# Converting float64 weights in place and between the parts of the attention: retention and a PReLU block on one core

## The chip, the cores and the metric

The kernel runs on one core of a Trainium2 chip. The metric is device time in microseconds: the median of the runs shown, and for the profiled execution its own time and its span (first to last instruction). Engines are TensorE (PE; its weight loads PEld), VectorE (DVE), ScalarE (ACT), GpSimd (POOL) and SyncE (SP), which here issues all transfers.

## The reference

```python
# q, k, v: (8, 8, 576, 64) float32: batch, heads, positions, head size
scores = q @ k.T / sqrt(64)
gamma = 1 - 2 ** (-5 - h)                       # one per head h
ret = scores * where(i >= j, gamma ** (i - j), 0)
x = (ret @ v)  rearranged to (4608, 512)        # batch*position, head*size
h = x @ w_in                                    # w_in (512, 2048), float64
g = max(h, 0) + alpha * min(h, 0)               # alpha (2048)
out = float32(g @ w_out)                        # w_out (2048, 512), float64
```

`w_in` and `w_out` arrive as float64 and are turned into float32 on the chip by integer operations on their two halves. All matrix products are float32.

## The kernel before

**Attention.** Work goes in 16 "couples" n: a batch b and four heads (u = 0 or 1), each with 4 blocks of 128 positions and a remainder of 64. Decay is put into `q` and `v` by tables (`tab`, `tabr`), products on GpSimd (L311, L313), so that scores need only a triangular mask. A couple runs `transposes` (TensorE `pt`, `ptr`, copied by ScalarE to `kT`, `qT`, `rT`), `scores` (`ps`, `psr`, masked by VectorE into `at`, `atr`), `states` (`pu`, added up by VectorE in `sums`) and `values` (`pv`, `pvr`, copied by ScalarE into `xb`).

**MLP.** A unit is 256 tokens (block kb) by a pair of 128-wide slices of the hidden layer (i = 0 to 7): 16 matmul records `ph` (L268), VectorE's PReLU and combinations `neg`, `g` (L276 to L284), 14 records `po` (L256) with a seven-product scheme. There are 18 x 8 = 144 units. `po` of a unit is issued after `ph` of the next. The last unit of a block ends in `out_block`, which combines the seven products and stores 256 rows. Units are taken from `queue` at three places of a couple; couples 2 and 3 take 2 and 4, couples 0 and 1 none, later ones what has become ready.

**Weights.** They come in 32 pieces of 512 KB, eight (a "stage": four of `w_in`, four of `w_out`) in each of couples 0 to 3. A piece is loaded to `raw` (three buffers), then: ScalarE takes Abs of the high words (L197, `wa`) and converts the low words (L199, `wl`); GpSimd clamps `wa` (L201); VectorE shifts it into the PSUM tile `wc` (L205) and joins it with the sign bits into `wb` (L207); GpSimd adds `wb` and `wl` into the weight tile (L209). After two `w_out` pieces, four subtractions (L222: two on VectorE, two on GpSimd) form the combined weights.

**What sets the order.** The program text gives priorities, a scheduler orders each engine's queue at build time, and each queue runs in order. Buffers rotate: pool `ps_a` has three PSUM buffers, shared by `pt`, `ptr`, `ps`, `psr`, `pu`, `pv`, `pvr` and every `wc`. All eight pieces of a stage are issued between `states` and `values`. The function around these lines, as it stands before:

Of the kernel before, what the change touches and what calls it, by code (L numbers as in the profile page):

```python
# [18 lines left out]
def kernel(  # L19
# [79 lines left out]
    pbi = const.tile([P, NBIT], INT32, name="pbi")
    for i in range(NBIT):  # L100
        nc.vector.tensor_scalar(pbi[:, i:i + 1], pint, i, 1,
                                ALU.logical_shift_right, ALU.bitwise_and)
# [3 lines left out]
    facr = const.tile([P, 2, NC2, 2], FP32, name="facr")
    gpw = const.tile([P, NBIT, H], FP32, name="gpw")
    for h in range(H):
        for i in range(NBIT):
            nc.gpsimd.memset(gpw[:, i, h:h + 1], float(np.float32(gam[h] ** 2 ** i)) - 1.0)  # L110
    for h in range(H):
        for j in range(NJ):
            nc.vector.memset(fac[:, 0, j, h:h + 1], gam[h] ** (j * C - MID) / np.sqrt(D))
            nc.vector.memset(fac[:, 1, j, h:h + 1], gam[h] ** (MID - j * C))
    for u in range(NC2):
        for i in range(2):
            for h2 in range(2):
                g_ = gam[4 * u + 2 * i + h2]
                rows = slice(i * REM, (i + 1) * REM)
                at_ = NJ * C - i * REM - MID  # L120
                nc.gpsimd.memset(facr[rows, 0, u, h2:h2 + 1], g_ ** at_ / np.sqrt(D))
                nc.gpsimd.memset(facr[rows, 1, u, h2:h2 + 1], g_ ** -at_)
    pw = const.tile([P, 2, H], FP32, name="pw")
    pwt = const.tile([P, H], FP32, name="pwt")
    for i in range(NBIT):
        t_ = pw[:, 0, :] if i == 0 else pwt
        nc.vector.tensor_scalar(t_, gpw[:, i, :], pbit[:, i:i + 1], 1.0, ALU.mult, ALU.add)
        if i:
            nc.vector.tensor_tensor(out=pw[:, 0, :], in0=pw[:, 0, :], in1=pwt, op=ALU.mult)
    nc.vector.reciprocal(pw[:, 1, :], pw[:, 0, :])  # L130
# [3 lines left out]
    for x in range(2):  # L134
        for u in range(NC2):
            hs = slice(4 * u, 4 * u + 4)
            nc.vector.tensor_tensor(out=tab[x][:, u], in0=fac[:, x, :, hs],
                                    in1=pw[:, x:x + 1, hs].to_broadcast([P, NJ, 4]),
                                    op=ALU.mult)
        for i in range(2):  # L140
            rows = slice(i * REM, (i + 1) * REM)
            nc.vector.tensor_tensor(
                out=tabr[rows, x], in0=facr[rows, x],
                in1=pw[rows, x].rearrange("p (u i h) -> p u i h", u=NC2, i=2)[:, :, i, :],
                op=ALU.mult)
# [317 lines left out]
```

## Time and profile before

| | us |
|---|---|
| median of 3 runs (lowest, highest) | 1233.37 (1233.04, 1235.24) |
| profiled execution | 1234.44 |
| its span | 1232.7 |
| TensorE busy | 1134.6 (92%) |
| VectorE, GpSimd, ScalarE busy | 565.1, 191.1, 112.5 |

The profile's page gives busy shares over 40 slices of 30.8 us; TensorE's are low in the first six and full after that, GpSimd's are high in the first six and low after that. A busy share over the whole span therefore says little about the first 190 us, and that stretch is read from views of its own: busy time by stretch, waits, groups of instructions and single rows in order of time. In those rows the number after a line and an operation is what the profile holds for it: "x32" instructions, busy time, mean in ns, and idle time of the engine before them with its releaser.

### The profile page before, as it was taken

To read this page: it belongs to the slowest core of one execution; us is meant where nothing else is said; L and a number is where in the kernel's file an instruction comes from. 1 tells how busy PE (TensorE), PEld (TensorE's weight loads), DVE (VectorE), ACT (ScalarE), POOL (GpSimd) and SP (SyncE) were. 2 spreads that over 40 slices of the span, in tenths; PEclk is the share of its full clock that TensorE was granted. 3 is DMA by queue.
4 is the path that set the end of the run, shared out by engine and by line. 5 is a ranking of instruction groups with operands and counts; after the bars stand their busy time and mean duration, and the time that the engine had idled before them with its cause. 6 is when DMAs were issued, how large, how long until landed. Compare 5 with 4: busy or idle time off the path is not lost.

```text
span 1232.7 us, 16093 instructions
## 1 busy us (share of the span) xinstructions
PE 1134.6 (92%) x6529; PEld 984.7 (80%) x6529; DVE 565.1 (46%) x1535; ACT 112.5 (9%) x283; POOL 191.1 (16%) x226
## 2 busy tenths in 40 slices
PE   2236779999999999999999999999999999999998
PEld 2135658888888888888888888888888888888887
DVE  5445565534535444454453444444444444444344
ACT  1242321000000000000000000000000000000000
POOL 5977862000000000000000000000000000000000
PEclk9567889999999999999999999999999999999999
DMA  7555431101011111111010111111110000000000
GB/s 174 152 164 150 131 103 41 35 20 40 23 31 40 37 39 37 25 33 37 22 35 20 39 37 39 37 39 38 39 38 13 6 1 18 1 17 18 1 18 18
DMA packets 127146, 55.58 MB, mean 45 GB/s; under 512 B 116304, under 2 KB 116320, under 8 KB 127072
## 3 DMA queue, kind: packets, MB, share of 16 engines
q1 hardware_dynamic: 127072, 54.56, 16.6%
q8 instruction: 51, 0.84, 0.3%
q14 instruction: 23, 0.19, 0.0%
HBM read 45.10 MB, written 9.44 MB: 44 GB/s over the span
## 4 chain that ended last, share of the span: by engine, by line
PE 86%; POOL 5%; DVE 3%; DMA 2%; SPq 2%; issue 1%; ACT 1%; DVEq 0%; POOLq 0%; ACTq 0%
PE ph L268 40%; PE po L256 34%; POOL wa L201 3%; PE ps L342 3%; PE pv L394 2%; PE pt L324 2%; PE pv L385 2%; DMA raw<-in_moe_w_in_dram 2%; PE pu L365 1%; SPq L76 1%; DVE at L346 1%; POOL w_out L209 1%; SPq L81 1%; PE psr L353 1%; DVE wb L207 1%
## 5 line engine op out<-in xcount | busy, mean ns | idle before, releaser
L268 PE MATMUL ph<-xb,w_in 128*128 128x256 f32 x2304 | 538.7, 385 | 17.1 <-DVE g L278 17.1
L268 PEld LDWEIGHTS ph<-xb,w_in 128*128 128x128 f32 x2304 | 436.1, 192 | 79.9 <-DVE g L278 12.1
L256 PE MATMUL po<-w_out,g 128*128 128x256 f32 x2016 | 458.5, 379 | 0.0
L256 PEld LDWEIGHTS po<-w_out,g 128*128 128x128 f32 x2016 | 383.0, 190 | 52.1
L276 DVE TENSOR_SCALAR neg<-ph,alpha 128x256 f32<-128x256 f32 x288 | 126.3, 479 | 522.5 <-PE ph L268 522.5
L284 DVE TENSOR_TENSOR g<-g 128x128 f32<-128x128 f32 x576 | 156.1, 311 | 8.7
L278 DVE SCALAR_TENSOR_TENSOR g<-ph,neg 128x512 f32<-128x512 f32 x144 | 99.5, 691 | 4.9
L313 POOL TENSOR_TENSOR vn<-vn,tab 128x1024 f32<-128x1024 f32 x16 | 30.4, 1903 | 428.1 <-DMA vn<-in_v_dram 337.7
L385 PE MATMUL pv<-at,vn 128*64 128x128 f32 x512 | 37.7, 306 | 52.0 <-DVE wb L207 52.0
L385 PEld LDWEIGHTS pv<-at,vn 128*64 128x64 f32 x512 | 32.3, 155 | 58.7 <-issue 49.9
L313 POOL TENSOR_TENSOR qn<-qn,tab 128x1024 f32<-128x1024 f32 x16 | 30.6, 1913 | 273.4 <-DMA qn<-in_q_dram 240.6
L201 POOL TENSOR_SCALAR wa<-wa 128x512 f32<-128x512 f32 x32 | 61.3, 1920 | 16.9 <-ACT wa L197 16.9
L346 DVE TENSOR_TENSOR at<-ps,mask 128x512 f32<-128x512 f32 x64 | 41.2, 686 | 43.9 <-PE ps L342 43.9
L303 ACT COPY xb<-pv 128x256 f32<-128x256 f32 (+3 forms) x88 | 21.8, 322 | 394.4 <-PE pv L394 394.3
L342 PE MATMUL ps<-qT,kT 64*128 64x128 f32 x512 | 48.0, 285 | 3.0 <-DVE at L346 1.5
L342 PEld LDWEIGHTS ps<-qT,kT 64*128 64x128 f32 x512 | 41.9, 187 | 11.0 <-DVE at L346 6.0
L327 ACT COPY kT<-pt 128x512 f32<-128x512 f32 x32 | 17.8, 592 | 296.6 <-PE pt L324 296.4
L205 DVE TENSOR_SCALAR wc<-wa 128x512 int32<-128x512 int32 x32 | 21.9, 692 | 42.7 <-POOL wa L201 42.7
L239 ACT COPY s<-po 128x256 f32<-128x256 f32 x18 | 6.7, 372 | 326.8 <-PE po L256 326.8
L374 DVE TENSOR_TENSOR sums<-pu,sums 64x128 f32<-64x128 f32 x96 | 27.7, 289 | 2.8
L394 PE MATMUL pv<-qT,sums 128*128 128x128 f32 x192 | 28.3, 302 | 0.0
L394 PEld LDWEIGHTS pv<-qT,sums 128*128 128x128 f32 x192 | 25.1, 209 | 3.1 <-issue 3.1
(64 smaller groups left out, 432.1 us busy)
## 6 DMA issues: line engine op xcount, KB each, us to landing
out_dram<-osb SPq DMA_DIRECT2D x36, 256.0 KB, 2.2
qn<-in_q_dram SPq DMA_DIRECT2D x64, 128.0 KB, 2.7
kn<-in_k_dram SPq DMA_DIRECT2D x64, 128.0 KB, 2.8
vn<-in_v_dram SPq DMA_DIRECT2D x64, 128.0 KB, 2.8
raw<-in_moe_w_in_dram SPq DMA_DIRECT2D x16, 512.0 KB, 4.5
raw<-in_moe_w_out_dram SPq DMA_DIRECT2D x16, 512.0 KB, 4.3
qr<-in_q_dram SPq DMA_DIRECT2D x32, 32.0 KB, 2.3
kr<-in_k_dram SPq DMA_DIRECT2D x32, 32.0 KB, 2.1
```

Source lines behind the costliest of these rows:

```text
L201: nc.gpsimd.tensor_scalar(a, a, HI_MIN, HI_MAX, ALU.max, ALU.min)
L256: nc.tensor.matmul(acc[kb][n // 2][:, n % 2, :], g[:, x, :], w_out[i][:, y, :], start=(i == 0 and n % 2 == 0), stop=(i == NU - 1 and (n % ...
L268: nc.tensor.matmul(ph[:, x, :], w_in[i // UST][:, cc, x, f0:f0 + P], xb[kb][:, cc, :], start=(cc == 0), stop=(cc == NCC - 1))
L276: nc.vector.tensor_scalar(neg[:, x], ph[:, x], 0.0, alpha[:, fc:fc + 1], ALU.min, ALU.mult)
L278: nc.vector.scalar_tensor_tensor(out=g[:, 0:4, :].rearrange("p x t -> p (x t)"), in0=ph.rearrange("p x t -> p (x t)"), scalar=0.0, in1=neg ...
L284: nc.vector.tensor_tensor(out=g[:, o, :], in0=g[:, x, :], in1=g[:, y, :], op=op)
L313: nc.gpsimd.tensor_tensor(out=t, in0=t, in1=tab[x][:, u, :, :, None].to_broadcast([P, NJ, 4, D]), op=ALU.mult)
L342: nc.tensor.matmul(ps[h2][:, cols], kT[i][rows, cols], qT[i][rows, cols], start=True, stop=True)
L346: nc.vector.tensor_tensor(out=a, in0=ps[h2].rearrange("p (j w) -> p j w", w=C), in1=mask[:, None, :].to_broadcast([P, NJ, C]), op=ALU.mult)
L374: nc.vector.tensor_tensor(out=sm[hd, j, :, hd], in0=ps[hd, j, :, :], in1=sm[hd, j - 1, :, hd], op=ALU.add)
L385: nc.tensor.matmul(pv[i][h2 * D:(h2 + 1) * D, j * C:(j + 1) * C], vn[:, j, 2 * i + h2, :], at[2 * i + h2][:, j, :], start=(j == 0), stop=F ...
L394: nc.tensor.matmul(pv[i][:, j * C:(j + 1) * C], sm[:, j - 1, i, :], qT[i][:, j * C:(j + 1) * C], start=False, stop=(j == NJ - 1), skip_gro ...
```

## The change

- A piece keeps its low words in `raw` (ScalarE writes them back in place), the clamp is VectorE's, the join writes into the weight tile, and GpSimd adds the low words there. `wb` and `wl` are gone; `raw` has four buffers, `wa` three.
- The pieces stand in a list, and a couple issues two after `transposes`, three after `scores` (and the first units) and three after `values`.
- The decay tables come from repeated squares and products on VectorE, where single memsets stood on VectorE and GpSimd; the remainder mask is built on GpSimd.
- `k` is loaded before `q`. The output tiles take the `raw` and `wa` buffers, both halves of a block in one tile.

```diff
-        for name, src in (("q", q), ("k", k), ("v", v)):
+        for name, src in (("k", k), ("q", q), ("v", v)):
...
+    for i in range(NBIT):
+        nc.vector.scalar_tensor_tensor(out=dif[:, i + 1], in0=dif[:, i], scalar=2.0,
+                                       in1=dif[:, i], op0=ALU.add, op1=ALU.mult)
...
-        raw = wraw.tile([P, 2, HM, 2], INT32, tag="raw", bufs=3, name=f"raw_{at}")
+        raw = wraw.tile([P, 2, HM, 2], INT32, tag="raw", bufs=4, name=f"raw_{at}")
         nc.sync.dma_start(raw, src)
...
+        lo, hi = raw[:, :, :, 0], raw[:, :, :, 1]
+        a = wraw.tile([P, 2, HM], FP32, tag="wa", bufs=3, name=f"wa_{at}")
+        nc.scalar.activation(a, hi.bitcast(FP32), ACTF.Abs)
+        nc.scalar.activation(lo, lo.bitcast(UINT32), ACTF.Copy, scale=2.0 ** -29)
-        nc.gpsimd.tensor_scalar(a, a, HI_MIN, HI_MAX, ALU.max, ALU.min)
+        nc.vector.tensor_scalar(a, a, HI_MIN, HI_MAX, ALU.max, ALU.min)
...
-        nc.vector.scalar_tensor_tensor(out=bi, in0=flat[:, :, 1], scalar=-0x40000000, in1=c,
-                                       op0=ALU.bitwise_and, op1=ALU.bitwise_or)
-        nc.gpsimd.tensor_tensor(out=dst.bitcast(INT32),
-                                in0=bi.rearrange("p (x f) -> p x f", x=2),
-                                in1=l.rearrange("p (x f) -> p x f", x=2), op=ALU.add)
+        nc.vector.scalar_tensor_tensor(
+            out=dst.rearrange("p x f -> p (x f)").bitcast(INT32),
+            in0=raw.rearrange("p x f two -> p (x f) two")[:, :, 1], scalar=-0x40000000,
+            in1=c.rearrange("p x f -> p (x f)"), op0=ALU.bitwise_and, op1=ALU.bitwise_or)
+        nc.gpsimd.tensor_tensor(out=dst.bitcast(INT32), in0=dst.bitcast(INT32), in1=lo,
+                                op=ALU.add)
...
+    def load_weights(n):
+        for _ in range(min(n, len(pieces))):
+            src, dst, unit = pieces.pop(0)
+            load_piece(src, dst)
+            if unit is not None:
+                combine(unit)
...
-        osb = [wraw.tile([P, 2, HM], FP32, tag="wa", name=f"osb{m}_{kb}") for m in range(2)]
-        s12 = wraw.tile([P, 2, HM], FP32, tag="wb", name=f"s12_{kb}")
-        u3 = wraw.tile([P, HM], FP32, tag="wl", name=f"u3_{kb}")
+        osb = wraw.tile([P, 2, 2, HM], FP32, tag="raw", bufs=4, name=f"osb_{kb}")
+        s12 = wraw.tile([P, 2, HM], FP32, tag="wa", bufs=3, name=f"s12_{kb}")
+        u3 = wraw.tile([P, HM], FP32, tag="wa", bufs=3, name=f"u3_{kb}")
...
         qT, kT, rT = transposes(n, b, u, tiles)
+        load_weights(2)
         pop_units(share // 3)
         at = scores(n, qT, kT, rT)
+        load_weights(3)
         states(n, tiles)
-        if n < NST:
-            load_stage(n)
         pop_units(share // 3)
         values(n, b, u, tiles, qT, rT, at)
+        load_weights(3)
         pop_units(share - 2 * (share // 3))
```

How the queues change, at three places. VectorE in couple 1, before, from the last remainder product (`atr`) on; `wc` and `wb` are the two vector steps of a piece, `sums` the states:

```order
L355 TENSOR_TENSOR atr_1_677<-psr_1_675,maskr 128x128
L205 TENSOR_SCALAR wc_712<-wa_706 128x512
L205 TENSOR_SCALAR wc_724<-wa_718 128x512
L372 COPY sums<-pu_679 64x2x64 x2
L374 TENSOR_TENSOR sums<-pu_679,sums 64x2x64 x6
L207 SCALAR_TENSOR_TENSOR wb_707<-raw_704,wc_712 128x512
```

The same engine in couple 1 of the changed kernel, from the end of the second piece on (L193 is the clamp, `wa` its tile, `at` the masked scores):

```order
L199 SCALAR_TENSOR_TENSOR w_in_186<-raw_516,wc_522 128x512
L193 TENSOR_SCALAR wa_564<-wa_564 128x512
L193 TENSOR_SCALAR wa_574<-wa_574 128x512
L349 TENSOR_TENSOR at_1_536<-ps_1_526,mask 128x512
L349 TENSOR_TENSOR at_1_538<-ps_1_527,mask 128x512
L193 TENSOR_SCALAR wa_584<-wa_584 128x512
L349 TENSOR_TENSOR at_1_550<-ps_1_540,mask 128x512
L349 TENSOR_TENSOR at_1_552<-ps_1_541,mask 128x512
```

Two pieces now end ahead of the masked scores and three clamps stand among them, where all of a couple's pieces followed the scores before.

SyncE, before, between the end of couple 0 and couple 1 (loads of couple 2's `k` and `v`, and the first pieces of stage 1):

```order
L76 DMA kn_0_590<-in_k_dram 128x4x64 x4
L81 DMA kr_0_591<-in_k_dram 64x2x64 x2
L189 DMA raw_704<-in_moe_w_in_dram 128x2x512
L76 DMA vn_0_598<-in_v_dram 128x4x64 x4
L81 DMA vr_0_599<-in_v_dram 64x2x64 x2
L189 DMA raw_716<-in_moe_w_in_dram 128x2x512
```

SyncE in the changed kernel, at the same place:

```order
L76 DMA kn_0_445<-in_k_dram 128x4x64 x4
L76 DMA vn_0_461<-in_v_dram 128x4x64 x4
L81 DMA vr_0_462<-in_v_dram 64x2x64 x2
L186 DMA raw_506<-in_moe_w_in_dram 128x2x512
L186 DMA raw_516<-in_moe_w_in_dram 128x2x512
```

The first piece of the stage stood ahead of `vn` and `vr`; now it stands behind them.

TensorE, before, from the end of couple 3's values to the first transpose of couple 4 (`ph_5` is the sixth unit, `g_4` the fifth unit's PReLU):

```order
L399 MATMUL pvr_1433<-rT_1187,sums 128x64 x2
L268 MATMUL ph_5_1493<-xb_568,w_in_308 128x256 x4
L256 MATMUL po_0_1144<-w_out_314,g_4_1477 128x256 x2
L256 MATMUL po_0_1145<-w_out_314,g_4_1477 128x256 x2
L256 MATMUL po_0_1146<-w_out_314,g_4_1477 128x256 x2
L256 MATMUL po_0_1147<-w_out_314,g_4_1477 128x256
L324 MATMUL pt_4_1551<-ident,kn_0_1163 128x128 x4
```

TensorE in the changed kernel, at the same place:

```order
L402 MATMUL pvr_1210<-rT_1018,sums 128x64 x2
L259 MATMUL po_0_975<-w_out_192,g_3_1192 128x256 x2
L259 MATMUL po_0_976<-w_out_192,g_3_1192 128x256 x2
L259 MATMUL po_0_977<-w_out_192,g_3_1192 128x256 x2
L259 MATMUL po_0_978<-w_out_192,g_3_1192 128x256
L327 MATMUL pt_4_1366<-ident,kn_0_986 128x128 x4
```

The sixth unit's `ph` and the fifth unit's `po` have moved behind couple 4's transposes.

## Rows read from the trace of the kernel before

**Rows 1.** Busy time by stretch: PE, PEld, DVE, ACT, POOL, PEclk, DMA share, GB/s

```profile
0.00:62.84 62.84, 16.74 (x140) 14.81 (x140) 29.08 (x131) 15.34 (x26) 44.40 (x112) 0.72 0.62 161
62.84:104.22 41.38, 16.65 (x143) 14.18 (x144) 17.81 (x34) 16.74 (x32) 35.44 (x26) 0.62 0.53 158
104.22:143.75 39.53, 27.70 (x183) 22.02 (x184) 22.30 (x47) 12.96 (x26) 30.47 (x22) 0.81 0.50 141
143.75:194.46 50.71, 41.19 (x259) 34.02 (x259) 32.56 (x63) 13.50 (x32) 35.06 (x28) 0.90 0.39 105
194.46:1226.00 1031.54, 1030.04 (x5802) 898.01 (x5801) 460.65 (x1253) 53.58 (x169) 45.70 (x40) 1.00 0.10 27
```

**Rows 2.** Waits of 20 to 195 us: who waited for whom, total, times, longest

```profile
PE pv L385 <- DVE wb L207: 52.0, 5, 26.0
```

**Rows 3.** Waits of SyncE's queue, 20 to 190 us

```profile
SPq L189 <- DVE wb L207: 60.6, 23, 5.2
```

**Rows 4.** Groups of instructions, 20 to 195 us: busy us, mean ns, idle before

```profile
L201 POOL TENSOR_SCALAR wa<-wa 128x512 f32<-128x512 f32 x32 | 61.3, 1920 | 16.9 <-ACT wa L197 16.9
...
L205 DVE TENSOR_SCALAR wc<-wa 128x512 int32<-128x512 int32 x32 | 21.9, 692 | 42.7 <-POOL wa L201 42.7
L207 DVE SCALAR_TENSOR_TENSOR wb<-raw,wc 128x512 int32<-128x512 int32 x32 | 21.6, 683 | 1.8 <-POOL w_in L209 1.2
...
L209 POOL TENSOR_TENSOR w_in<-wb,wl 128x512 int32<-128x512 int32 x16 | 20.1, 1270 | 4.3 <-DVE wb L207 4.3
...
L284 DVE TENSOR_TENSOR g<-g 128x128 f32<-128x128 f32 x24 | 11.8, 517 | 0.3
...
L346 DVE TENSOR_TENSOR at<-ps,mask 128x512 f32<-128x512 f32 x15 | 9.7, 685 | 16.3 <-PE ps L342 16.3
...
L374 DVE TENSOR_TENSOR sums<-pu,sums 64x128 f32<-64x128 f32 x24 | 6.9, 289 | 0.7
L276 DVE TENSOR_SCALAR neg<-ph,alpha 128x256 f32<-128x256 f32 x12 | 5.5, 478 | 6.4 <-PE ph L268 6.4
...
L278 DVE SCALAR_TENSOR_TENSOR g<-ph,neg 128x512 f32<-128x512 f32 x6 | 4.1, 690 | 0.2
```

**Rows 5.** Single instructions in order of time: start, duration, engine, line

```profile
4.07 1.21 DVE L127 TENSOR_SCALAR pwt<-gpw,pbit 128x8 f32<-128x8 f32 x1
...
4.29 0.97 POOL L158 MEMSET sums<- 128x1024 f32 x1
...
5.53 0.23 DVE L152 COPY maskr<-mask 128x128 f32<-128x128 f32 x1
...
46.48 1.90 POOL L313 TENSOR_TENSOR qn<-qn,tab 128x1024 f32<-128x1024 f32 x1
...
46.56 2.10 DVE L222 TENSOR_TENSOR w_out<-w_out 128x256 f32<-128x256 f32 x1 [0.54 <-POOL w_out L209]
...
50.70 0.43 DVE L222 TENSOR_TENSOR w_out<-w_out 128x256 f32<-128x256 f32 x1 [1.44 <-POOL w_out L209]
```

**Rows 6.** Tile `raw` (ns: min/median/max, first and last start), and one stretch

```profile
L197 ACT ACTIVATE wa<-raw x32: 658/668/711, 27.3 to 179.0; 128x512 f32<-128x512 f32 x32
...
L189 SPq DMA_DIRECT2D raw<-in_moe_w_in_dram x16: 540/567/612, 22.8 to 163.6; - x16
...
DMA to landing us min/median/max: 3.2/4.4/7.2
...
20.00:30.00 10.00, 2.64 (x46) 2.15 (x46) 4.43 (x14) 1.44 (x3) 4.18 (x3) 0.87 0.82 225
```

**Rows 7.** TensorE in order of time, and on the chain of work

```profile
13.70 0.26 PE L164 MATMUL aps<-ident,a 16*128 16x16 f32 x1 [13.70 <-DMA a<-in_moe_alpha_dram]
...
59.37 2.93 PE L394 MATMUL pv<-qT,sums 128*128 128x128 f32 x12
...
203.25 3.45 PE ph L268 x16
206.70 3.02 PE po L256 x14
```

More of the change, by code (lines that the diff above doesn't have):

```diff
@@ new lines @@
+    for h in range(H):
+        nc.vector.memset(dif[:, 0, h:h + 1], gam[h] - 1.0)
+    for h in range(H):
+        nc.vector.memset(fac[:, 0, h:h + 1], gam[h] ** -MID / np.sqrt(D))
+    for i in range(NBIT):
+        nc.vector.scalar_tensor_tensor(out=dif[:, i + 1], in0=dif[:, i], scalar=2.0,
+                                       in1=dif[:, i], op0=ALU.add, op1=ALU.mult)
+    facl = const.tile([P, 2, H], FP32, name="facl")
+    for o, y, i in [(fac[:, j], fac[:, j - 1], NBIT) for j in range(1, NJ)] + \
+            [(facl[:, i], fac[:, NJ - 1], NBIT - i) for i in range(2)]:
+        nc.vector.scalar_tensor_tensor(out=o, in0=dif[:, i], scalar=1.0, in1=y,
+                                       op0=ALU.add, op1=ALU.mult)
@@ L98 @@
+    nc.vector.tensor_tensor(out=pbi, in0=pint, in1=pbi, op=ALU.logical_shift_right)
+    nc.vector.tensor_scalar(pbi, pbi, 1, None, ALU.bitwise_and)
     pbit = const.tile([P, NBIT], FP32, name="pbit")
[L99 to L102, printed above, removed]
     nc.vector.tensor_copy(pbit, pbi)
-    fac = const.tile([P, 2, NJ, H], FP32, name="fac")
@@ L106 @@
[L106 to L130, printed above, removed]
+    pf = const.tile([P, NBIT, H], FP32, name="pf")
+    nc.vector.tensor_tensor(out=pf, in0=dif[:, 0:NBIT],
+                            in1=pbit[:, :, None].to_broadcast([P, NBIT, H]), op=ALU.mult)
@@ L132 @@
+    nc.vector.tensor_scalar(pf, pf, 1.0, None, ALU.add)
+    pw = pf[:, 0]
+    for o, x in ((pf[:, 0:3], pf[:, 3:6]), (pw, pf[:, 1]), (pw, pf[:, 2]), (pw, pf[:, 6])):
+        nc.vector.tensor_tensor(out=o, in0=o, in1=x, op=ALU.mult)
     tab = [const.tile([P, NC2, NJ, 4], FP32, name=f"tab{x}") for x in range(2)]
     tabr = const.tile([P, 2, NC2, 2], FP32, name="tabr")
[L134 to L145, printed above, removed]
+    for u in range(NC2):
+        hs = slice(4 * u, 4 * u + 4)
+        nc.vector.tensor_tensor(out=tab[0][:, u], in0=fac[:, :, hs],
+                                in1=pf[:, 0:1, hs].to_broadcast([P, NJ, 4]), op=ALU.mult)
@@ L147 @@
+    for i in range(2):
+        rows = slice(i * REM, (i + 1) * REM)
+        x, y = [t_.rearrange("p (u i h) -> p u i h", u=NC2, i=2)[:, :, i, :]
+                for t_ in (facl[rows, i], pw[rows])]
+        nc.vector.tensor_tensor(out=tabr[rows, 0], in0=x, in1=y, op=ALU.mult)
+    for o, x in ((tabr[:, 1], tabr[:, 0]), (tab[1], tab[0])):
+        nc.vector.tensor_scalar(o, x, float(np.sqrt(D)), None, ALU.mult)
+        nc.vector.reciprocal(o, o)
     mask = const.tile([P, C], FP32, name="mask")
@@ L151 @@
     maskr = const.tile([P, C], FP32, name="maskr")
-    nc.vector.tensor_copy(maskr, mask)
-    nc.vector.memset(maskr[0:REM, REM:C], 0.0)
+    nc.gpsimd.tensor_copy(maskr, mask)
+    nc.gpsimd.memset(maskr[0:REM, REM:C], 0.0)
     sm = const.tile([P, NJ, 2, P], FP32, name="sums")
@@ L214, in load_stage, with combine @@
+        nc.gpsimd.tensor_tensor(out=dst.bitcast(INT32), in0=dst.bitcast(INT32), in1=lo,
+                                op=ALU.add)
+    def combine(i):
+        w = w_out[i]
+        for eng, o, x, y in ((nc.vector, 4, 1, 0), (nc.vector, 5, 3, 4),
+                             (nc.gpsimd, 6, 5, 2), (nc.gpsimd, 1, 3, 1)):
+            eng.tensor_tensor(out=w[:, o], in0=w[:, x], in1=w[:, y], op=ALU.subtract)
+    pieces = []
+    for s in range(NST):
         for cc in range(NCC):
-            load_piece(win32[cc, :, :, s * FS:(s + 1) * FS, :], w_in[s][:, cc])
+            pieces.append((win32[cc, :, :, s * FS:(s + 1) * FS, :], w_in[s][:, cc], None))
@@ L216, in load_stage @@
         for i in range(UST * s, UST * (s + 1)):
[L217 to L222 removed]
+            pieces.append((wout32[i], w_out[i][:, 0:2], None))
+            pieces.append((wout32[NU + i], w_out[i][:, 2:4], i))
@@ L377, in values @@
     def values(n, b, u, tiles, qT, rT, at):
-        qn, qr, kn, kr, vn, vr = tiles
+        kn, kr, qn, qr, vn, vr = tiles
         x0 = b * S
```

42 lines of the change are left out of this document (15 added, 27 removed).

## The prediction, made before the changed kernel ran

> **What bounds the kernel now.** I read the busy time per stretch first, cut where TensorE begins the transposes of couple 1, 2, 3 and 4 [rows 1]. After 194.46 us TensorE is busy 1030.04 of 1031.54 us at full clock: nothing in that stretch can be shortened by other engines, and the change leaves the arithmetic there alone. Before 194.46 it is busy 102 us (16.74 + 16.65 + 27.70 + 41.19), part of it at the lower clock. So whatever this change is worth lies in the first 194 us, where the float64 weights become float32.
>
> The waits of that stretch say why TensorE stands: 52.0 us in its `pv` matmuls (L385) for the vector step that ends a conversion (L207), and VectorE stands 42.7 us for GpSimd's clamp (L201) [rows 2, 4]. The mechanism is in the code: `wc` of every piece and every attention tile rotate through the three buffers of `ps_a`, all eight pieces of a couple are issued between `pu` and `pv`, so `pv` gets its buffer only after the eighth. GpSimd sets their pace: clamp 1.920 plus add 1.270 us a piece [rows 4], 8 x 3.19 = 25.5 us a couple beside its other work, so that it is busy 35.44 and 30.47 us in couples of 41.38 and 39.53 [rows 1]. SyncE stands 60.6 us for the same L207 step, because the raw buffer is free only then [rows 3]: three buffers and a landing of 4.4 us [rows 6] leave the transfers waiting too.
>
> **Part 1, the clamp moves to VectorE.** It takes 61.3 us off GpSimd [rows 4]. On VectorE 512 elements cost between 0.25 and 0.69 us: a copy of 128 columns between SBUF tiles takes 0.23 [rows 5], the two-operation form of 512 columns that writes PSUM 0.692 [rows 4]. I take 0.5, between the two, since the copy's own rate is well below a nanosecond a column. GpSimd keeps what [rows 1] show less eight clamps, 35.44 - 15.4 and 30.47 - 15.4, on the mean 17.6 us a couple. It is not next in line.
>
> But the trace shows a price. At 4.07 VectorE's tensor_scalar between SBUF tiles took 1.21 us for 8 columns, more than five times the 128-column copy, and ended with GpSimd's memset of 4.29 to 5.26; at 46.56 a subtraction took 2.10 where the one at 50.70 took 0.43, beside GpSimd's product of 46.48 to 48.38 [rows 5]. So the clamp, the same form, can stand for a GpSimd instruction, up to 1.7 us. With GpSimd busy 17.6 of some 32 us it meets one in 55% of cases and waits half of 1.3 to 1.9: about 0.4 us each, 3.4 us a couple. Bounds: 0 and 8 x 1.7 = 13.6.
> The Trainium skill (SBUF — State Buffer, section "SBUF: two separate sides") says the pair of ports that both engines share is an exclusive lock, held for a whole instruction by whichever began first; these rows agree with it. By it alone, with every clamp late by a whole instruction, the gain would be gone: that is rival 2.
>
> **Part 2, conversion in place.** ScalarE's two passes stay (0.67 us each [rows 6]); the second writes back into `raw` at an 8-byte step. The add on GpSimd now reads that half at the same step, and adds into the weight tile. No row shows a GpSimd read at a step; ScalarE reads `raw` at that step in 0.668 us [rows 6] and VectorE in 0.683, no slower than its plain form of 0.692 [rows 4], so I take 1.27 and keep 2.5 (twice) as the other end; at 2.5 GpSimd has 27.4 us a couple, still below the length I arrive at, and the buffer comes back 1.2 us later. The buffer's release moves from L207 to the add: later by 1.3 us per round trip. The fourth buffer outweighs that.
>
> **Part 3, the pieces stand in three groups** (two behind the transposes, three behind the scores, three behind `pv`). TensorE now meets a conversion at three places, none longer than three pieces. VectorE's queue becomes the chain: the order of couple 1 shows two clamps ahead of the first mask product and one ahead of the third, each behind a transfer. I add up couple 1 on VectorE:
> - 8 pieces x (0.5 + 0.692 + 0.683) = 15.0 us
> - 4 mask products x 0.685 = 2.7; ten small ones (six `sums`, two copies, two of the remainder) x 0.289 = 2.9; 4 subtractions x 0.43 = 1.7 [rows 4, 5]
>
> Together 22.3 us. Then its waits. (a) The fourth piece takes a buffer freed by the add of the last piece of the couple before: add 1.3 + issue 0.6 + landing 4.4 + Abs 0.7 = 6.9 us [rows 4, 6], in which VectorE has two pieces and a clamp, 4.3 us: 2.6 exposed. (b) The fifth piece needs the first one's buffer: the same 6.9 us, mostly behind that: 1.5. (c) Between `sums` and the third group stand `pvr`, twelve `pv` matmuls (2.93 at the lower clock [rows 7]) and ScalarE's copy, 4.2 us, of which a clamp and a subtraction hide 0.9: 3.3. (d) The port, 3.4. Sum 22.3 + 2.6 + 1.5 + 3.3 + 3.4 = 33; the transposes lie beside (a). I take 32, since (a) and (d) partly overlap, against 41.38 now.
>
> Couples 2 and 3 have two MLP units each in VectorE's queue: 2 x 0.478 + 0.690 + 4 x (0.28 to 0.517) = 2.8 to 3.7, say 3.2 us a unit [rows 4], 6.5 for both, which hides (a) and (b), 4.1: 34.4 each. TensorE needs 15 to 17 us of attention there (couple 0's 16.74; couple 3's 41.19 less four units of 6.5 [rows 1, 7]) and 2 x 6.5 for the units: 28 to 30, below 34.
>
> Couple 0: the first raw issue stays at 22.8, the first Abs at 27.3 [rows 6]. The fourth piece now leaves at once: 4 x 0.524 MB at 225 GB/s is 9.3 us [rows 6], so its Abs falls near 34; mask products with the fifth clamp between them to 40, three pieces and `sums` to 47, (c) to 51, the third group to 55. Couple 1 begins at 55 instead of 62.84.
>
> So couple 4 begins at 55 + 32 + 34.4 + 34.4 = 155.8 instead of 194.46: 38.7 us earlier. What is late next is TensorE itself, but with more to do: the order has five units' `ph` and four units' `po` ahead of couple 4's transposes where six and five stood, so 3.45 + 3.02 = 6.5 us [rows 7] move behind it. Gain 38.7 - 6.5 = 32.2.
>
> **Part 4, tables, loads, output.** TensorE's first instruction is the transpose of alpha, which waits for its transfer at 13.70 [rows 7]; the alpha load stays behind 18 loads in SyncE's queue, so neither the new tables (some thirty small vector operations, each near the small copy's 0.23 us [rows 5], 7 us in all) nor loading `k` first move it: 0, bounds -0.3 to +0.3. The output tiles take the `raw` and `wa` buffers once a block, eight units or 52 us apart on a saturated TensorE: 0.
>
> **Sum.** The profiled execution took 1234.44 us, 1.1 above the median of the runs shown (1233.37); its span is 1232.7. 1234.4 - 32.2 = 1202.2, by the median 1201 us, which I give.
>
> **Rivals.**
> 1. *The waits vanish.* If transfers land in 3.2 us (the fastest row [rows 6]) and the clamp costs 0.25, (a), (b) and (d) go. The floor is the bytes: 8 x 0.524 + 1.77 for q, k, v = 5.96 MB a couple, 26.5 us at 225 GB/s. Couple 4 then begins at 54 + 3 x 26.5 = 133.5: 1180. With 28 to 30 us: 1184 to 1190. Against it: SyncE's queue puts the first raw load of a couple behind `vn` and `vr`, which wait for `pv`.
> 2. *The port takes the gain.* Every clamp stands 1.7 us: 10 us more in each couple, 35 in all: 1235, no change. A half of that: 1217. For it: GpSimd's adds follow VectorE's step closely, so a clamp meets the add of the piece before. Against it: GpSimd idles 40%.
> 3. *Slower: the three groups wait in lockstep.* Each group pays issue, landing and Abs in full, 5.6 us, since buffers return only after the add and raw loads stand in order behind loads that wait for TensorE: 16.8 us instead of 4.1, 12.7 more in couples 1 to 3 and 3 in couple 0. Couple 4 begins at 197; 1242. It decides from a mean of 44 us per couple on (55 + 3 x 44.4 = 194.46 - 6.5). Against it: four buffers, and two clamps that run ahead of the masks.
>
> **Chances.** The forecast, 1188 to 1214: 0.55. Rival 1, 1180 to 1188: 0.13. Between forecast and rival 2, 1214 to 1231: 0.20. No change, within 0.2% (2.5 us, about what a measurement of this kernel can tell): 0.04. Rival 3: 0.08. The range 1180 to 1224 leaves out the tail of rival 2, no change and rival 3.
>
> **What would show it.** Right: TensorE's wait for conversions falls from 52 us to parts below 8 each; GpSimd busy near 18 us a couple; couple 4's transposes near 156; a stretch behind them as dense as now. Wrong: clamps of mean over 1.2 us (rival 2); SyncE's waits for the add near 60 us and couples over 44 (rival 3); GpSimd's add near 2.5; or TensorE idle after couple 4 has begun, which no step here allows for.

## The result, and the profile after

The changed kernel takes 1199.05 us (median; 1198.50 to 1200.99). The kernel before took 1233.43 beside it, so the ratio is 0.972 (95% interval 0.970 to 0.974): 34.4 us faster. The forecast was 1201, and the profiled executions stand 35.9 us apart (1234.44 and 1198.50) where the sum said 32.2.

One identity orders everything that follows: span = TensorE's busy time + its idle time.

| | before | after |
|---|---|---|
| span | 1232.7 | 1196.8 |
| TensorE busy | 1134.6 | 1135.9 |
| TensorE idle | 98.1 | 60.9 |
| GpSimd busy | 191.1 | 131.0 |
| VectorE busy | 565.1 | 584.5 |

The idle time fell by 37.2 us and the busy time rose by 1.3. Where it fell is seen in the busy time by stretch, cut again where TensorE begins the transposes of couples 1, 2, 3 and 4 (length; busy time of PE, PEld, DVE, ACT, POOL with records; PEclk; DMA share; GB/s). These rows answer [rows 1]:

```profile
0.00:50.39 50.39, 19.12 (x144) 16.48 (x144) 23.02 (x82) 14.54 (x28) 20.51 (x28) 0.76 0.67 176
50.39:81.37 30.98, 20.39 (x150) 17.07 (x151) 23.13 (x43) 14.03 (x28) 19.23 (x17) 0.67 0.75 196
81.37:114.64 33.27, 28.17 (x198) 22.47 (x196) 29.75 (x55) 14.35 (x30) 18.15 (x17) 0.90 0.71 187
114.64:149.06 34.42, 29.07 (x200) 22.80 (x201) 30.36 (x60) 13.96 (x29) 19.14 (x17) 0.90 0.74 184
149.06:1190.10 1041.04, 1036.87 (x5832) 904.07 (x5831) 475.59 (x1271) 53.58 (x169) 53.99 (x49) 1.00 0.10 26
```

Couple 4 begins at 149.06 instead of 194.46, 45.4 us sooner. The stretch behind it is 9.5 us longer (1041.04 against 1031.54), and 45.4 - 9.5 = 35.9 is the whole gain. GpSimd's share of a couple has fallen to 18 to 19 us; VectorE is now busy 23 of 31, 30 of 33 and 30 of 34 us in couples 1 to 3.

The waits between 20 and 165 us (who waited for whom; total, times, longest) answer [rows 2, 3]:

```profile
ACT wa L189 <- DMA raw<-in_moe_w_out_dram: 35.5, 11, 5.8
DVE wa L193 <- ACT wa L189: 18.5, 7, 13.9
ACT wa L189 <- DMA raw<-in_moe_w_in_dram: 16.4, 11, 8.9
...
PE ps L345 <- DVE w_in L199: 14.4, 3, 11.1
...
PE pt L327 <- DVE w_out L199: 4.5, 2, 4.2
```

```profile
SPq L186 <- POOL w_in L203: 41.1, 13, 7.3
SPq L186 <- POOL qr L314: 11.1, 3, 4.6
SPq L186 <- POOL w_out L203: 7.8, 7, 2.7
...
SPq L186 <- POOL w_out L210: 2.3, 3, 1.6
```

TensorE's 52.0 us in `pv` are gone (1.6 are left). It now stands in `ps`, once for 11.1 us in couple 0, and in `pt`. SyncE's waits ahead of raw loads have hardly changed: 60.6 us in [rows 3], and 41.1 + 11.1 + 7.8 + 2.3 = 62.3 here, now all put down to GpSimd, whose add (L203) frees the buffer. The gain is therefore not that SyncE waits less. The groups of instructions between 20 and 165 us (busy us, mean ns, idle before) answer [rows 4]:

```profile
L193 DVE TENSOR_SCALAR wa<-wa 128x512 f32<-128x512 f32 x32 | 20.6, 645 | 18.5 <-ACT wa L189 18.5
...
L203 POOL TENSOR_TENSOR w_in<-w_in,raw 128x512 int32<-128x512 int32 x16 | 21.2, 1325 | 37.1 <-DVE w_in L199 14.8 <-ACT wa L189 13.3 <-ACT raw L191 4.9
...
L388 PE MATMUL pv<-at,vn 128*64 128x128 f32 x128 | 9.9, 313 | 1.6 <-DVE w_out L199 1.6
```

### The profile page after: what moved, and what is told of

It is laid out like the page before. It is cut to its first block, busy times and chain, and to the rows that moved or that the text cites. A ratio compares the mean times of both kernels' runs of the same rounds, so it can differ in the third digit from the quotient of the medians.

```text
span 1196.8 us, 15945 instructions
## 1 busy us (share of the span) xinstructions
PE 1135.9 (95%) x6529; PEld 984.5 (82%) x6529; DVE 584.5 (49%) x1516; ACT 110.8 (9%) x283; POOL 131.0 (11%) x125
## 3 DMA queue, kind: packets, MB, share of 16 engines
q1 hardware_dynamic: 127072, 54.56, 17.6%
## 4 chain that ended last, share of the span: by engine, by line
PE 88%; DVE 3%; DMA 1%; issue 0%; POOL 0%; SPq 0%; DVEq 0%; POOLq 0%
PE ph L271 42%; PE po L259 35%; PE ps L345 2%; PE pv L388 2%; PE pv L397 2%; PE pt L327 2%; PE pu L368 1%; DVE at L349 1%; PE psr L356 1%; DMA vn<-in_v_dram 1%; PE pvr L402 0%; DVE w_out L210 0%; DVE wa L193 0%; PE pvr L392 0%; DMA qr<-in_q_dram 0%
## 5 line engine op out<-in xcount | busy, mean ns | idle before, releaser
L287 DVE TENSOR_TENSOR g<-g 128x128 f32<-128x128 f32 x576 | 162.7, 323 | 8.6
L345 PE MATMUL ps<-qT,kT 64*128 64x128 f32 x512 | 55.9, 304 | 18.5 <-DVE w_in L199 14.4
L345 PEld LDWEIGHTS ps<-qT,kT 64*128 64x128 f32 x512 | 48.1, 203 | 28.5 <-DVE w_in L199 15.4
L330 ACT COPY kT<-pt 128x512 f32<-128x512 f32 x32 | 17.6, 590 | 294.4 <-PE pt L327 294.2
L388 PE MATMUL pv<-at,vn 128*64 128x128 f32 x512 | 33.6, 285 | 1.6 <-DVE w_out L199 1.6
L388 PEld LDWEIGHTS pv<-at,vn 128*64 128x64 f32 x512 | 29.5, 144 | 6.1 <-issue 4.0
L193 DVE TENSOR_SCALAR wa<-wa 128x512 f32<-128x512 f32 x32 | 20.6, 645 | 18.5 <-ACT wa L189 18.5
L189 ACT ACTIVATE wa<-raw 128x512 f32<-128x512 f32 x32 | 21.5, 672 | 55.5 <-DMA raw<-in_moe_w_out_dram 35.5
L397 PEld LDWEIGHTS pv<-qT,sums 128*128 128x128 f32 x192 | 23.1, 191 | 4.2 <-issue 2.7
```

Of the source, the lines that this page charges most:

```text
L287: nc.vector.tensor_tensor(out=g[:, o, :], in0=g[:, x, :], in1=g[:, y, :], op=op)
L345: nc.tensor.matmul(ps[h2][:, cols], kT[i][rows, cols], qT[i][rows, cols], start=True, stop=True)
L388: nc.tensor.matmul(pv[i][h2 * D:(h2 + 1) * D, j * C:(j + 1) * C], vn[:, j, 2 * i + h2, :], at[2 * i + h2][:, j, :], start=(j == 0), stop=F ...
L397: nc.tensor.matmul(pv[i][:, j * C:(j + 1) * C], sm[:, j - 1, i, :], qT[i][:, j * C:(j + 1) * C], start=False, stop=(j == NJ - 1), skip_gro ...
```

## The experiments

Times are medians of four executions each; a ratio is to the kernel before, timed beside it on the same chip. In three series it took 1234.10, 1233.57 and 1232.19 us, so kernels of different series are compared by their ratios. The first series holds the clamp on GpSimd, the bunched pieces, three buffers and the old tables; the second the two parts alone, the clamp twice and the clamp into PSUM; the third the rest. Differences in us below are between the medians as they stand: scaled to the kernel before of its series, a kernel would be 0.7 us lower in the first, 0.1 lower in the second and 1.2 higher in the third. The split of a span is that of the profiled execution.

| kernel | time, us | ratio (95%) | TensorE busy | idle |
|---|---|---|---|---|
| before | 1233.43 | 1 | 1134.6 | 98.1 |
| after | 1199.05 | 0.972 (0.970 to 0.974) | 1135.9 | 60.9 |
| clamp only | 1215.21 | 0.985 (0.983 to 0.986) | 1130.3 | 82.5 |
| spread only | 1213.58 | 0.984 (0.982 to 0.985) | 1136.8 | 75.2 |
| after, clamp on GpSimd | 1214.90 | 0.985 (0.983 to 0.986) | 1137.2 | 75.7 |
| after, pieces bunched | 1208.52 | 0.979 (0.977 to 0.980) | 1130.7 | 78.6 |
| after, three raw buffers | 1211.39 | 0.982 (0.980 to 0.983) | 1141.0 | 68.7 |
| after, old tables | 1199.84 | 0.973 (0.971 to 0.975) | 1136.8 | 60.3 |
| after, clamp twice | 1218.27 | 0.987 (0.986 to 0.989) | 1141.8 | 75.2 |
| after, clamp into PSUM | 1212.24 | 0.983 (0.981 to 0.984) | 1136.5 | 72.0 |
| after, loads later | 1206.23 | 0.979 (0.977 to 0.980) | 1142.0 | 64.3 |
| after, five raw buffers | 1198.24 | 0.972 (0.971 to 0.974) | 1135.9 | 60.8 |
| after, both of these | 1205.00 | 0.978 (0.977 to 0.980) | 1141.0 | 64.2 |
| after, pieces 3, 3, 3 | 1206.29 | 0.980 (0.978 to 0.981) | 1138.1 | 66.4 |

### What each part is worth

**The clamp back on GpSimd.** Theory: the clamp's place carries about half of the gain.

```diff
-        nc.vector.tensor_scalar(a, a, HI_MIN, HI_MAX, ALU.max, ALU.min)
+        nc.gpsimd.tensor_scalar(a, a, HI_MIN, HI_MAX, ALU.max, ALU.min)
```

> The changed kernel with the clamp back on GpSimd, all else as changed. Theory (GpSimd's 3.2 us a piece set the pace): GpSimd gets 8 x 1.92 = 15.4 us more a couple, 34.5 in all, couples lengthen from 31 to 34 to about 38, couple 4 begins near 168, time about 1218 us. Rival (the spreading of the pieces is what counts, the clamp's engine is beside the path): at most 5 us more, 1199 to 1204.

Measured 1214.90, 15.9 above the changed kernel. The group of the clamp and VectorE's wait for it, in this kernel's trace (groups as above from 20 to 200 us; waits from 20 to 165 us):

```profile
L193 POOL TENSOR_SCALAR wa<-wa 128x512 f32<-128x512 f32 x32 | 61.5, 1930 | 11.4 <-ACT wa L189 6.8 <-DMA qn<-in_q_dram 4.6
```

```profile
DVE w_out L210 <- POOL w_out L203: 30.8, 12, 5.6
DVE wc L197 <- POOL wa L193: 26.2, 11, 16.1
```

The 61 us of GpSimd are back, and so is VectorE's wait for them (42.7 before [rows 4], 26.2 here). VectorE's wait for GpSimd's add ahead of the subtractions (L210) has grown as well, from 11.4 us in the changed kernel to 30.8. The theory held.

**The clamp alone, in the kernel before.** The same line the other way round, and nothing else.

```diff
-        nc.gpsimd.tensor_scalar(a, a, HI_MIN, HI_MAX, ALU.max, ALU.min)
+        nc.vector.tensor_scalar(a, a, HI_MIN, HI_MAX, ALU.max, ALU.min)
```

> The kernel before with the clamp on VectorE, all else as before (pieces bunched, three raw buffers freed by the join, two of each work tile). Theory (GpSimd's pace was the larger of the two causes): about 15 us gained, as the opposite edit lost 15.9: 1215 to 1222 us. Rival (the two causes only pay together): 1228 or more.

Measured 1215.21, which is 18.4 us faster than before. Its waits from 20 to 165 us:

```profile
PE pv L385 <- DVE wb L207: 49.1, 8, 21.2
...
PE ph L268 <- DVE g L278: 8.0, 2, 6.1
```

In the kernel before, the second of these waits was longer (20 to 195 us):

```profile
PE ph L268 <- DVE g L278: 17.1, 4, 6.2
```

TensorE stands in `pv` nearly as long as before (52.0 us): the conversions are still one block ahead of `pv`. The couples are shorter all the same (55.4, 34.3, 37.3 and 47.9 us against 62.8, 41.4, 39.5 and 50.7). Of the 15.6 us of idle time that are gone, 9.1 show in the wait of `ph` for VectorE's `g`, which stands in the same queue as the conversions.

**The order alone, in the kernel before.** Pieces are put in a list and issued two, three and three; the conversion stays as it was.

```diff
+        load_weights(2)
...
+        load_weights(3)
         states(n, tiles)
-        if n < NST:
-            load_stage(n)
...
+        load_weights(3)
```

> The kernel before with the pieces issued two, three and three among the parts of the attention, all else as before. Theory (GpSimd's 3.2 us a piece is the pace whatever the place): GpSimd stays busy 33 to 35 us a couple, couples near 38, time 1222 to 1230 us. Rival (the place alone unlocks the gain): under 1212.

Measured 1213.58, 20 us faster than before: between the two expectations, and more than the theory gave. The busy tenths of GpSimd, 40 slices of the span, first this kernel and then the changed one:

```profile
POOL 5898980000000000000000000000000000000000
```

```profile
POOL 3565430000000000000000000000000000000000
```

GpSimd is busy eight tenths or more from the second slice to the sixth, and couples 1 to 3 last 38.6, 41.3 and 39.5 us here, near the 38 of the theory. Couples 1 and 2 together gained 1.0 us against [rows 1]; the gain is in couple 0 (51.9 instead of 62.8) and in couple 3 (39.5 instead of 50.7). So GpSimd's pace held, but the time that the theory named left out how much longer than 38 us couples 0 and 3 had been.

**The changed kernel with all eight pieces ahead of `values`.**

```diff
-        load_weights(2)
...
-        load_weights(3)
         states(n, tiles)
+        load_weights(8)
...
-        load_weights(3)
```

> The changed kernel with all eight pieces of a couple issued between states and values again. Theory (both the pace and the place count: TensorE's pv waits for eight pieces at 2.5 to 3 us each): couples about 37, couple 4 near 164, time about 1213 us. Rival (once GpSimd is free the place does not matter): 1199 within 3 us. A second rival: bunched is better, since VectorE's queue then never stands for a clamp ahead of a mask product: 1190.

Measured 1208.52, 9.5 above the changed kernel; the theory said 1213, the rivals 1199 and 1190. The waits from 20 to 200 us show the old one again:

```profile
PE pv L388 <- DVE w_out L199: 38.8, 7, 18.3
```

**Three raw buffers instead of four.**

```diff
-        raw = wraw.tile([P, 2, HM, 2], INT32, tag="raw", bufs=4, name=f"raw_{at}")
+        raw = wraw.tile([P, 2, HM, 2], INT32, tag="raw", bufs=3, name=f"raw_{at}")
...
-        osb = wraw.tile([P, 2, 2, HM], FP32, tag="raw", bufs=4, name=f"osb_{kb}")
+        osb = wraw.tile([P, 2, 2, HM], FP32, tag="raw", bufs=3, name=f"osb_{kb}")
```

> The changed kernel with three raw buffers instead of four. Theory (the round trip of a buffer, some 8.5 us, limits: 2.8 us a piece with three against 2.1 with four): 5 to 6 us more a couple, about 20 in all, 1219 us. Rival (VectorE's own 23 us a couple is the limit, the buffer only a small wait): 5 us more at most, 1199 to 1204.

The output tiles take the same buffers, so their line changes with it. Measured 1211.39, 12.3 above: about midway between the theory's 1219 and the upper end of the rival's range, 1204. Waits from 20 to 165 us:

```profile
ACT wa L189 <- DMA raw<-in_moe_w_in_dram: 40.9, 15, 8.5
ACT wa L189 <- DMA raw<-in_moe_w_out_dram: 33.2, 11, 8.0
DVE wa L193 <- ACT wa L189: 24.8, 11, 13.5
```

ScalarE waits 74.1 us for landings instead of 51.9. With three buffers the whole change gives 22 us, hardly more than the order alone (20), and with four it gives 34. A likely reason is that in place a buffer returns only behind the add. That is not shown: no run has the clamp and the order without conversion in place, so what conversion in place costs or gains by itself stays open.

**The old tables in the changed kernel** (the table code of before, the rest unchanged).

```diff
-        nc.vector.memset(dif[:, 0, h:h + 1], gam[h] - 1.0)
...
+        for i in range(NBIT):
+            nc.gpsimd.memset(gpw[:, i, h:h + 1], float(np.float32(gam[h] ** 2 ** i)) - 1.0)
```

> The changed kernel with the decay tables built as before (single memsets on VectorE and GpSimd). Theory (TensorE's first instruction waits for alpha at 13.8 us whatever the tables do): 1199 within 1 us. Rival (the squares and products free GpSimd or VectorE early enough to matter): 2 us or more above.

Measured 1199.84: the tables carry nothing that can be measured.

### What bounds the changed kernel

**The clamp issued twice.** The second clamp changes no value; it adds one VectorE instruction to each piece.

```diff
         nc.vector.tensor_scalar(a, a, HI_MIN, HI_MAX, ALU.max, ALU.min)
+        nc.vector.tensor_scalar(a, a, HI_MIN, HI_MAX, ALU.max, ALU.min)
```

> The changed kernel with the clamp issued twice on the same tile (the second changes nothing): 8 x 0.43 to 0.65 us more VectorE work a couple, 3.4 to 5.2. Theory (VectorE's queue is the chain of a couple): nearly all of it shows, 12 to 18 us over four couples, 1211 to 1217 us. Rival (the landing of transfers is the chain, VectorE's 18.5 us of waiting for Abs absorbs it): 1199 to 1204.

Measured 1218.27, 19.2 above the changed kernel and 1.3 above the theory's range. The second clamps, in groups from 20 to 165 us (two of the 32 start later):

```profile
L194 DVE TENSOR_SCALAR wa<-wa 128x512 f32<-128x512 f32 x30 | 20.0, 670 | 0.4
```

32 x 0.670 = 21.4 us were added to VectorE's queue (its busy time rose by 18.9, from 584.5 to 603.4), couple 4 begins 18.4 us later (167.44), and the time is 19.2 longer. A second clamp also keeps its raw buffer that much longer; but a fifth buffer, below, brings couple 4 only 2.7 us forward, so in the main it is VectorE's queue that is the chain, as the prediction said. TensorE's idle time rose by 14.3 only; its busy time rose by 5.9 for the same 6529 records, at a lower clock (0.78 on the mean between 13.5 and 200 us against 0.84 in the changed kernel; more on this below).

**The clamp into PSUM.** The clamp writes `wc`, and the shift works on `wc` in place. The question was what the clamp loses by standing for GpSimd.

```diff
-        nc.vector.tensor_scalar(a, a, HI_MIN, HI_MAX, ALU.max, ALU.min)
         c = ps_a.tile([P, 2, HM], INT32, tag="psa", name=f"wc_{at}")
-        nc.vector.tensor_scalar(c, a.bitcast(INT32), 3, 0x3FFFFFF8,
+        nc.vector.tensor_scalar(c.bitcast(FP32), a, HI_MIN, HI_MAX, ALU.max, ALU.min)
+        nc.vector.tensor_scalar(c, c, 3, 0x3FFFFFF8,
```

> The changed kernel with the clamp writing into the PSUM tile that the shift then reads and overwrites. It then has one SBUF operand. Theory (the clamp of mean 0.645 us is 0.43 of work and 0.22 of standing for GpSimd, most of it in a few of 1 to 2 us): each takes 0.69 without a long one, in sum the same 22 against 20.6 us; a PSUM buffer is held 0.7 us longer a piece; time 1199 to 1205 us, longest clamp under 0.8. Rival (GpSimd does not hold it up; the long ones come from something else): clamps over 1 us remain.

The durations came out as expected, the time did not: 1212.24, 13.2 above. The clamp in this kernel, and below it the clamp of the changed kernel (ns: min/median/max; first and last start):

```profile
L196 DVE TENSOR_SCALAR wc<-wa x32: 682/686/696, 28.1 to 156.2; 128x512 f32<-128x512 f32 x32
```

```profile
L193 DVE TENSOR_SCALAR wa<-wa x32: 411/427/2127, 28.1 to 146.7; 128x512 f32<-128x512 f32 x32
```

Into PSUM no clamp is late, but each takes 0.69 us, so the mean got worse (0.645 before the edit) by 1.4 us in all. What else changed is the order: the clamp now needs one of the three PSUM buffers of `ps_a`, an instruction sooner, and VectorE waits for ScalarE's copies, which free such buffers (20 to 165 us; in the changed kernel no such wait is listed):

```profile
DVE wc L196 <- ACT xb L306: 10.8, 4, 4.8
```

VectorE's rows in this kernel, with the wait ahead of the third group of couple 0:

```profile
46.38 0.43 DVE L210 TENSOR_TENSOR w_out<-w_out 128x256 f32<-128x256 f32 x1 [1.63 <-POOL w_out L203]
51.61 1.29 DVE L196 TENSOR_SCALAR wc<-wa 128x512 f32<-128x512 f32 x2 [4.80 <-ACT xb L306]
```

The changed kernel runs the clamp of that place at 47.77, ahead of ScalarE's copies, since it needs no PSUM. ScalarE in turn has two pieces queued ahead of those copies here, and one in the changed kernel; it waits 7.96 us for the first of the two to land (5.83 there). So this run doesn't price the standing for GpSimd: it takes away one wait and brings in another.

**Couple n+1's loads behind the first two pieces.** TensorE's longest wait (11.1 us, in couple 0) stands behind the first raw piece, which SyncE issues at 22.73 behind six groups of loads of couple 1.

```diff
-        if n + 1 < len(couples):
-            loaded[n + 1] = load_couple(*couples[n + 1])
...
         load_weights(2)
+        if n + 1 < len(couples):
+            loaded[n + 1] = load_couple(*couples[n + 1])
```

> The changed kernel with couple n+1's q, k, v loads issued behind the first two pieces of couple n, not ahead of them. In the trace of the changed kernel the first raw piece is issued at 22.73 us because six groups of loads of couple 1 stand before it on SyncE's queue (12.16 to 22.68), and TensorE idles from 19.0 to 30.1 behind it. Theory (couple 0 is held by the arrival of its first pieces): the first raw load goes out at about 12.2, couple 0 ends 6 to 9 us sooner (42 to 44 instead of 50.4), of which couple 1 may give one or two back, and the time is 1190 to 1194. Rival (the chain of 32 pieces on VectorE and their landing sets the pace from start to end, or couple 1's q and k come too late): 1197 to 1201.

Both expectations missed: 1206.23, some 8 us slower than the changed kernel by the ratios. The first raw load did go out at 12.15. TensorE's rows of couple 0 in this kernel (start, duration; in brackets the idle time before):

```profile
21.42 3.94 PE L345 MATMUL ps<-qT,kT 64*128 64x128 f32 x27 [2.01 <-DVE w_in L199]
...
35.08 1.97 PE L368 MATMUL pu<-vn,kn 128*64 128x64 f32 x32 [8.21 <-DVE w_in L199]
39.81 3.46 PE L388 MATMUL pv<-at,vn 128*64 128x128 f32 x32 [2.76 <-DVE w_in L199]
```

The scores' wait shrank from 11.1 to 2.0, and a wait of 8.2 came up in `pu`: two pieces are early, but the third now leaves at 27.73, behind the same loads. TensorE's idle time in couple 0 is 31.5 us here and 31.3 in the changed kernel. The wait was moved, not removed. Couple 3 is 4.3 us longer (38.76 against 34.42), for a reason that was not followed; in all, couple 4 begins 6.6 us later and the stretch behind it is 3.0 us longer.

**Five raw buffers.**

```diff
-        raw = wraw.tile([P, 2, HM, 2], INT32, tag="raw", bufs=4, name=f"raw_{at}")
+        raw = wraw.tile([P, 2, HM, 2], INT32, tag="raw", bufs=5, name=f"raw_{at}")
...
-        osb = wraw.tile([P, 2, 2, HM], FP32, tag="raw", bufs=4, name=f"osb_{kb}")
+        osb = wraw.tile([P, 2, 2, HM], FP32, tag="raw", bufs=5, name=f"osb_{kb}")
```

> The changed kernel with five raw buffers instead of four. In the changed kernel ScalarE waits 35.5 + 16.4 us for landings of raw pieces between 20 and 165 us, and three buffers instead of four cost 12.3 us. Theory (landings still set part of the pace): a part of that again, 1193 to 1197. Rival (four buffers cover the 4.6 us of a landing, and VectorE's queue alone is what is left): 1198 to 1201.

The output tiles' line changes with it, as above. Measured 1198.24, at 0.972 the ratio of the changed kernel: the rival's range. Couple 4 begins at 146.37, 2.7 us sooner than with four buffers, so the theory's gain was there. It went at once (TensorE's rows, first this kernel, then the changed one):

```profile
150.95 6.62 PE L271 MATMUL ph<-xb,w_in 128*128 128x256 f32 x16 [2.67 <-DVE g L281]
```

```profile
155.43 3.72 PE L271 MATMUL ph<-xb,w_in 128*128 128x256 f32 x16 [2.14 <-DVE g L281]
```

The same 16 matmul records take 6.62 us here and 3.72 there. The busy time of that stretch in the kernel with five buffers has the granted clock in the third column from the end (0.54; columns as above):

```profile
151.00:157.40 6.40, 6.40 (x16) 5.16 (x17) 2.51 (x5) 0.00 (x0) 1.86 (x3) 0.54 0.02 4
```

The lower level, 1.2 GHz, costs 2.9 us in this one place, as much as couple 4 had gained.

**Both edits**, the later loads and the fifth buffer, as in the two diffs above.

> Both: loads of couple n+1 behind the first two pieces, and five raw buffers. Theory (two separate limits, the first arrival and the depth): 1184 to 1190. Rival (one limit, both ease the same): the better of the two alone, 1190 to 1194. Second rival (VectorE's queue alone): 1197 to 1201.

Measured 1205.00, above all three expectations: by the ratios all of the loss of the later loads, and nothing from the fifth buffer.

**Three pieces in the first slot.** The pieces go 3, 3, 3, and couple 3 keeps five.

```diff
-        load_weights(2)
+        load_weights(3)
```

> The changed kernel with three pieces, not two, in the first slot of each couple (3, 3, 3 until the 32 are used up), so that couple 3 has five pieces left instead of eight. It asks after the 3.0 us that TensorE idles behind couple 4's start (2.1 of them waiting for VectorE's g while the last conversions stand in its queue). Theory (the last pieces in VectorE's queue make that idle): the last clamp comes some us before couple 4's start, the idle behind it falls below 1 us, and with the same work in all the time is 1195 to 1198. Rival (nine pieces in couples 0 to 2 lengthen these by more than couple 3 gains, as VectorE and the landings already fill them): 1200 to 1206.

Measured 1206.29, 0.3 above the rival's range. TensorE's stretch from couple 4 on, in this kernel:

```profile
167.18:1198.00 1030.82, 1029.46 (x5803) 897.95 (x5802) 465.57 (x1253) 53.57 (x170) 46.11 (x40) 1.00 0.10 27
```

Behind couple 4's start TensorE idles 1.4 us (1030.82 - 1029.46) against 4.2 in the changed kernel, which agrees with the theory's cause of that idle time: VectorE's last step for a piece (L210) now starts 13.5 us ahead of couple 4, where in the changed kernel it starts 4.9 us behind its beginning. It doesn't prove that cause, since this kernel also has one unit more ahead of couple 4 (5803 records behind its start against 5832). Couples 0 to 3 cost more than was gained (54.3, 38.6, 37.0, 37.3 us). No version beats the changed kernel by more than these measurements can tell.

## Why the prediction was right, step by step

**What bounded the kernel before.** Right. All of the gain is in the first 149 us, and each of the two causes that were named, GpSimd's pace and the block ahead of `pv`, is worth 18 to 20 us alone.

**Part 1, the clamp.** Taken as 0.5 of work and 0.4 for the port; measured 0.43 (the median) and 0.22 (mean 0.645 less the median): the sum's term of 0.9 was too large by 0.26 us a clamp. The mechanism can be seen in pairs of rows, VectorE's clamp and GpSimd's instruction beside it:

```profile
33.99 1.08 DVE L193 TENSOR_SCALAR wa<-wa 128x512 f32<-128x512 f32 x1 [0.36 <-ACT wa L189]
...
105.23 2.13 DVE L193 TENSOR_SCALAR wa<-wa 128x512 f32<-128x512 f32 x1
```

```profile
33.42 1.36 POOL L203 TENSOR_TENSOR w_in<-w_in,raw 128x512 int32<-128x512 int32 x1 [1.94 <-DVE w_in L199]
...
105.17 1.90 POOL L316 TENSOR_TENSOR qn<-qn,tab 128x1024 f32<-128x1024 f32 x1 [1.34 <-DMA qn<-in_q_dram]
```

GpSimd's two end at 34.78 and 107.07, the clamps at 35.07 and 107.36: 0.29 us later each time. A clamp that meets a GpSimd instruction waits for its end: 13 of the 32 clamps take over 0.5 us, and each of these ends 0.28 or 0.29 us behind the GpSimd instruction that ran when it began; the other 19 take 0.41 to 0.43. That is the exclusive lock of the Trainium skill (SBUF — State Buffer, section "SBUF: two separate sides"), and the trace agrees. So the sum's 55% of cases at 0.8 us were 41% at 0.54. Rival 2's mechanism is real, but its price was 0.22 of the 1.7 us it needed per clamp. GpSimd's share of a couple was 17.6 in the forecast and is 18.2 to 19.2 in couples 1 to 3.

**Part 2, in place.** GpSimd's add at the 8-byte step takes 1.31 to 1.33 us on the mean (1.27 taken, 2.5 kept as the other end). A fourth buffer is worth 12.3 us, by the run with three; what the later release costs was not run by itself, so that the one "outweighs" the other is not shown.

**Part 3, the couples.** Forecast 32, 34.4 and 34.4; measured 30.98, 33.27 and 34.42. The landing of 4.4 that the waits (a) and (b) rest on measured 4.6 (median; 3.3 to 8.5). The term that was mis-sized is couple 0: it ended at 50.39, not 55. The steps up to the states were right (masks to 39.3, forecast 40; `sums` to 45.9, forecast 47). Then the sum let the third group of pieces end ahead of couple 1. In the trace TensorE begins couple 1's transposes at 50.39, while the third group runs on VectorE from 47.8 to beyond 56, and pays 4.2 us for it inside couple 1 (the wait of `pt` above). What was counted as the end of one couple lies partly beside the next.

Couple 1 came out near its forecast, but not by its terms. VectorE is busy 23.1 of its 31.0 us (22.3 of work and 3.4 for the port were forecast), and nearly all of its idle time stands ahead of these instructions:

```profile
51.75 0.42 DVE L210 TENSOR_TENSOR w_out<-w_out 128x256 f32<-128x256 f32 x1 [0.87 <-POOL w_out L203]
...
54.21 0.93 DVE L210 TENSOR_TENSOR w_out<-w_out 128x256 f32<-128x256 f32 x1 [1.17 <-POOL w_out L203]
...
57.93 0.42 DVE L210 TENSOR_TENSOR w_out<-w_out 128x256 f32<-128x256 f32 x1 [1.46 <-POOL w_out L203]
59.12 0.79 DVE L193 TENSOR_SCALAR wa<-wa 128x512 f32<-128x512 f32 x1 [0.77 <-ACT wa L189]
...
67.69 0.43 DVE L193 TENSOR_SCALAR wa<-wa 128x512 f32<-128x512 f32 x1 [1.25 <-ACT wa L189]
...
78.04 0.43 DVE L210 TENSOR_TENSOR w_out<-w_out 128x256 f32<-128x256 f32 x1 [1.62 <-POOL w_out L203]
```

The four subtractions (L210) wait 0.87 + 1.17 + 1.46 + 1.62 = 5.1 us for GpSimd's add of their weights. The sum had no such term, though two rows of [rows 5] show this wait in the kernel before. The waits (a) and (b) for ScalarE's Abs are 0.77 + 1.25 = 2.0 us against 4.1. The wait (c) for ScalarE's copies, 3.3 in the sum, doesn't show: the clamp needs no PSUM buffer, and what stands ahead of the third group is the last of the four waits for GpSimd. So 7.4 us of waits (a) to (c) were forecast and 7.1 came, from other places: that VectorE's queue makes the length is right, that the number fits is in part luck.

"None longer than three pieces", and so no wait above 8 us, was wrong in one place: 11.1 us in `ps` of couple 0, behind the first piece to land.

**What goes behind couple 4.** 6.5 us of moved work were forecast; TensorE's busy time there rose by 6.8 (1036.87 - 1030.04). Not forecast is idle time: 4.2 us instead of 1.5. The prediction named just that as what would make it wrong. 2.1 us of it is the wait at 155.43, TensorE for VectorE's `g`, while the last pieces stand in VectorE's queue; it is not there in the run with 3, 3, 3. The prediction took the stretch to stay as dense as before.

**The sum.** Couple 4 came 6.7 us sooner than forecast (149.06, not 155.8) and the stretch behind it got 3.0 us longer than forecast: 32.2 + 6.7 - 3.0 = 35.9. Two errors of opposite sign; that the second took back nearly half of the first is luck.

**Part 4.** The tables are worth nothing (0.8 us between two medians whose executions spread over 2.5 and 5.2). That the output tiles cost nothing agrees with the dense last stretch. They were not tried alone, nor was loading `k` first.

**Rival 3** came to nothing with four buffers. With three, waits for landings grew by 22 us and the time by 12.3, so its mechanism is there, a step away. One of its two signs did show: SyncE waits 62.3 us for GpSimd, near the 60 that were named. The other, couples over 44 us, did not (31 to 34).

## What to carry to other kernels

When a chain of short steps feeds a saturated engine, cost it as the sum of the busiest queue per round, then count its neighbours' waits: here 21.4 us put into VectorE's queue came back as 19.2 in the time, and taking the clamp off the queue that held up the chain paid even though the new engine was the busier one over the whole span. The parts don't add up: the clamp alone gained 18 us, the order alone 20, the whole change 22 with three buffers and 34 with four. A total that fits doesn't vouch for its terms: look for each wait of the sum in the trace. Before a load is moved ahead, ask what leaves behind it: the wait of 11.1 us became one of 8.2 at the next place.
